# Attention and an ELU feed-forward layer on one core: weights loaded and decoded in pairs, and the first 64 queries of a pair turned by DMA

## The chip, the cores and the metric

The kernel runs on one core of one Trainium2 chip. The metric is the device time of one execution in microseconds; times of the kernel before are the median of three runs. Beside them there is one profiled execution, recorded by the hardware profiler, from which all durations below come.

## The reference

```python
def _attn_ref(q, k, v, s):                       # q, k, v: 8 batches, 8 heads, 576 positions, 64 wide
    scores = (1.0 / np.sqrt(D)) * np.matmul(q, k.transpose(0, 1, 3, 2))
    causal = np.triu(np.ones((S, S), dtype=bool), k=1)
    cum = np.cumsum(np.maximum(s, 0.0), axis=-1)
    bias = -(cum[:, :, :, None] - cum[:, :, None, :])
    scores = np.where(causal, -1000000000.0, scores + np.minimum(bias, 0.0))
    scores = scores - np.max(scores, axis=-1, keepdims=True)
    attn = np.exp(scores)
    attn = attn / (np.sum(attn, axis=-1, keepdims=True) + 1e-09)
    return np.matmul(attn, v)
...
x = attn_out.transpose(0, 2, 1, 3).reshape(8 * 576, 512)     # 4608 tokens
h = x @ w_in                                                 # 512 x 2048
g = np.where(h > 0.0, h, np.exp(np.minimum(h, 0.0)) - 1.0)
return g @ w_out                                             # 2048 x 512
```

All inputs are float32 and so is the output.

## The kernel before, in words

**The planner.** The program does not write its instructions in the order in which they run. It hands operations to a small planner (class `Plan`): each operation has a priority, its reads and writes, and one or more ways, that is an engine with an assumed cost. `issue` then takes, again and again, the operation that could start first by its own reckoning (ties by priority), chooses the way that ends first, and appends the instruction to that engine's program. So the order on every engine is fixed when the kernel is built, and each engine works it off in order. An operation's buffer is part of the reckoning: it cannot start before a slot of its pool is free. Until a planned time of 60 us (`FILL_T`) PE's gaps are filled by transpositions of the identity into a scratch bank (L1545, L1547).

**Three parts of the work.**

1. *Low units.* For batches 0 to 2, each of the four head pairs' first 320 positions are done in float32 products (`scoring_low` and `weighing_low`; tiles `sc`, `pl`, `trl`, `tl`, `avl`). Their x feeds the feed-forward layer's chunk 0.
2. *Later pairs.* The rest of the attention is done by `Unit`s with operands that are split into two float16 parts. A pair of heads has a unit for its first 64 queries ("None" in the names, both heads in one 128-row block; 20 of these in all) and one for each head's later queries. For a head's unit: scores (L1065), maximum and exponential (L1068 on DVE, L1073 on ACT), probabilities scaled and split in two parts (`halved`, L1119 to L1133), a DMA transposition T<-p (L409, issued on SP's queue), products with v (L1252: the two heads of a pair stand side by side, each 64 columns of the array), and an eviction with a scale (L1264 on ACT or L1266 on DVE) into x, which is stored to `x_dram`.
3. *The feed-forward layer*, 18 chunks of 256 tokens. Chunk 0 takes float32 products and the decoded weights `wa` (first layer L1423, second layer L1477); the other 17 take float16 parts, three products for each (first layer L1427, second L1484), from the split weights `wp`. A first-layer tile h covers two blocks of 128 hidden units; gg is its activation.

**The None units before the change.** The probabilities are normalised in float32 (`normalize`, L1086 to L1090: psh), transposed on PE (L1218: tr_None), split into two rounded parts (`split_pt`: copy L443 or L444, difference L1151), multiplied with the values' two rounded parts side by side (L1211, two products of 128 columns: av_None), and brought to x by four half evictions (`halves`: copies L443 or L444, additions L1280), two for each head.

**The weights.** They arrive as 64-bit words, a float32 in 8 bytes. `load_unit` takes one block of 128 hidden units of one matrix, 512 KB, in one of four slots of `raws` (32 loads, w_in and w_out in turn). Decoding is an ACT pass over the one half-word (L693), a mask on the other (L697 on DVE or L699 on ACT), and their union on DVE (L702: `wa`), then a maximum (L623 on DVE or L626 on ACT: `peaks`). After the last of them `weight_scales` makes the scales of both matrices, and `split_unit` makes the two parts of each block (the scaled high part L428 to L430; the low part L717 on DVE), at a priority of −500, ahead of nearly everything.

**Around it.** T has two buffers of its own, and two more where the last groups of `wa` lay once these are free. Score tiles may use the h banks while no more than the first nine h tiles have been opened. A later pair's operands are loaded, scaled, split, written to DRAM (`spread`) and read again (`set`). SP issues every one of these DMAs in one queue.

## Time and profile before

| | |
|---|---|
| median of the runs | 1038.81 us (1037.28 to 1039.48) |
| the profiled execution | 1034.6 us, of which its span 1032.8 us |
| PE busy | 1003.1 us, 97% of the span |
| DVE, ACT, POOL busy | 845.2 (82%), 669.0 (65%), 295.9 (29%) us |
| largest groups on PE | first layer 402.7 + 297.3 us, second layer 392.7 us (float16 parts; they overlap) |
| DMA moved | 179.83 MB, mean 174 GB/s |

Busy times are those of one profiled execution. A row of groups gives line, engine, operation and tiles, the count, then busy time and the mean of one in ns, and after the second bar the engine's idle time ahead of them and who ended it. PE's matmuls are pipelined, so a matmul's duration is longer than the distance to the next one; what one costs is read from the starts. "128*64" is the part of the array that is used. In the views PEld is the weight load, SPq a queue's issue.

### The profile page before, as it was taken

The numbers are of one execution on the slowest core, as the hardware profiler recorded it, in microseconds if no ns is written. First come the engines' busy times: TensorE is split into PE (matmuls) and PEld (weight loads), VectorE is DVE, ScalarE is ACT, GpSimd is POOL, SyncE is SP. The second block draws the span as 40 slices with busy tenths as digits, with TensorE's granted clock in tenths as the row PEclk, the third lists the DMA queues.
The fourth block names the chain that finished last, engine by engine and source line by source line (L and its number), as shares of the span: only waits on it lengthen the run. The fifth ranks groups of instructions, "written<-read, shape, count | busy, mean of one in ns | idle before, by whom it ended". The sixth has DMA issues, their size and how long they took to land. (4 is left out here: it accounts for less than half of the span.)

```text
span 1032.8 us, 21782 instructions
## 1 busy us (share of the span) xinstructions
PE 1003.1 (97%) x7305; PEld 688.7 (67%) x7305; DVE 845.2 (82%) x2346; ACT 669.0 (65%) x1559; POOL 295.9 (29%) x487
## 2 busy tenths in 40 slices
PE   8889999999999999999999999999999999999998
PEld 6667656676666666666666666676666676666665
DVE  7999998788988988898889999798988898863232
ACT  4898755666667766776776766666675765644343
POOL 6343452242323323241234242222232123100000
PEclk9999999999999999999999999999999999999999
DMA  7997524589979997999989987979998998841000
GB/s 197 276 289 236 150 72 95 124 190 213 222 166 212 207 192 165 198 202 208 196 174 201 232 179 174 229 181 192 215 198 196 227 202 187 182 94 47 1 21 21
DMA packets 296724, 179.83 MB, mean 174 GB/s; under 512 B 209908, under 2 KB 270564, under 8 KB 296612
## 3 DMA queue, kind: packets, MB, share of 16 engines
q1 hardware_dynamic: 296612, 178.45, 75.7%
q8 instruction: 57, 0.93, 0.4%
q14 instruction: 55, 0.45, 0.2%
HBM read 93.08 MB, written 36.81 MB: 126 GB/s over the span
## 5 line engine op out<-in xcount | busy, mean ns | idle before, releaser
L1427 PE MATMUL h<-xh,wp 128*128 128x256 f16 x2176 | 402.7, 273 | 0.7 <-DVE gg L1466 0.7
L1484 PE MATMUL o<-wp,gg 128*128 128x512 f16 x1632 | 392.7, 380 | 0.5 <-DVE gg L1466 0.5
L1427 PEld LDWEIGHTS <-wp 128*128 128x128 f16 x3264 | 317.4, 98 | 69.7 <-issue 2.1
L1427 PE MATMUL h<-xl,wp 128*128 128x256 f16 x1088 | 297.3, 273 | 1.1 <-DVE xl L1403 1.1
L1484 PEld LDWEIGHTS <-gg 128*128 128x128 f16 x1632 | 157.7, 98 | 144.5 <-DVE gg L1466 1.0
L1073 ACT ACTIVATE p<-p,mn 128x192 f32<-128x192 f32 (+1 forms) x232 | 143.7, 620 | 54.9 <-DVE mn L1068 52.9
L1133 DVE SCALAR_TENSOR_TENSOR p<-p,sm,p 128x512 f16<-128x512 f32 (+3 forms) x257 | 162.8, 662 | 4.9 <-POOL p L1125 2.4
L1459 DVE SCALAR_TENSOR_TENSOR h<-g,cs,h 128x512 f32<-128x512 f32 x136 | 102.0, 750 | 60.5 <-ACT g L1446 59.2
L1125 POOL TENSOR_SCALAR p<-p,sm 128x512 f16<-128x512 f32 (+3 forms) x94 | 65.1, 696 | 290.5 <-DVE sm L1079 117.1
L1439 ACT ACTIVATE g<-h,cs 128x512 f32<-128x512 f32 x136 | 92.8, 682 | 78.0 <-PE h L1427 77.2
L1463 ACT ACTIVATE gg<-h 128x512 f16<-128x512 f32 x132 | 78.3, 593 | 83.2 <-DVE h L1459 79.3
L1068 DVE CUSTOM_DVE_ANT_0 p<-sc,maskw 128x192 f32<-128x192 f32 (+1 forms) x232 | 109.5, 481 | 11.9 <-PE sc L1065 8.5
L1065 PE MATMUL sc<-set 128*128 128x288 f16 (+3 forms) x544 | 112.7, 299 | 4.5 <-DVE mn L1068 4.3
L1466 DVE SCALAR_TENSOR_TENSOR gg<-h,gg 128x512 f16<-128x512 f32 x136 | 93.3, 686 | 16.3 <-ACT gg L1463 15.7
L1129 ACT ACTIVATE p<-p,sm 128x512 f16<-128x512 f32 (+3 forms) x139 | 75.1, 557 | 19.0 <-DVE sm L1079 5.5
L1065 PEld LDWEIGHTS <-set 128*128 128x128 f16 x584 | 55.1, 98 | 41.6 <-issue 8.6
L1252 PE MATMUL av<-T,v 128*64 128x256 f16 (+5 forms) x960 | 62.4, 278 | 2.8 <-DMA T<-p 2.8
L1252 PEld LDWEIGHTS <-v 128*64 128x64 f16 x960 | 48.5, 110 | 23.3 <-issue 12.3
L1446 ACT ACTIVATE g<-g 128x512 f32<-128x512 f32 x81 | 50.9, 628 | 1.9
L428 POOL TENSOR_SCALAR v<-va,scales 128x320 f16<-128x320 f32 (+1 forms) x45 | 26.8, 599 | 64.9 <-PE av L1252 58.3
L1073 ACT ACTIVATION_READ_ACCUMULATOR p<-p,mn 128x1 f32 x232 | 43.7, 188 | 0.0
L1068 DVE CUSTOM_DVE_ANT_0 p<-sc,maskw,mn 128x288 f32<-128x288 f32 x64 | 32.9, 514 | 7.1 <-PE sc L1065 5.5
(200 smaller groups left out, 1261.0 us busy)
## 6 DMA issues: line engine op xcount, KB each, us to landing
set<-spread SPq DMA_DIRECT2D x32, 432.0 KB
spread<-parts_None SPq DMA_DIRECT2D x32, 288.0 KB
set<-spread SPq DMA_DIRECT2D x32, 288.0 KB
raws<-in_w_in_dram SPq DMA_DIRECT2D x16, 512.0 KB
raws<-in_w_out_dram SPq DMA_DIRECT2D x16, 512.0 KB
out_dram<-ost SPq DMA_DIRECT2D x32, 256.0 KB
va<-in_vb_dram SPq DMA_DIRECT2D x16, 352.0 KB
xc<-x_dram SPq DMA_DIRECT2D x22, 256.0 KB
```

Source lines behind the costliest of these rows:

```text
L1065: pe_.matmul(view(sc.v[:, :cw]), l, r, start=n == 0, stop=n == len(pairs) - 1)
L1068: op(prio, [("DVE", 84 + dve_p(cw), lambda i=i, sc=sc: dve.tensor_tensor_reduce(pt.v[:, i * cw : (i + 1) * cw], sc.v[:, :cw], mv(i * cw, c ...
L1073: op(prio, [("ACT", 480 + w / 1.2, lambda: act.activation(pt.v[:, :w], pt.v[:, :w], AF.Exp, bias=mn.v[:, n - 1 : n], scale=-1.0, accum_out ...
L1129: ("ACT", 295 + size / 1.2, lambda part=part: act.activation(part(0), own(part), AF.Copy, scale=sm.v[:, r])),
L1133: ("DVE-SB", dve_2(size), lambda part=part: dve.scalar_tensor_tensor(part(1), own(part), sm.v[:, r], part(0), ALU.mult, ALU.subtract)),
L1252: pe_.matmul(av.v[w.h * HB : (w.h + 1) * HB, dst], w.values.v[:, w.h, kb, v], part(w, kb, m), start=kb == 0 and m == 0 and v == 0, stop=kb ...
L1427: pe_.matmul(columns(k), weight_part(f, 0, part)[1]()[:, c * P : (c + 1) * P], xx.v[:, c], start=(c == 0 and m == 0), stop=(c == NCB - 1 a ...
L1439: op(side, [("ACT", act_c(W) + (0 if native else 90), lambda: act.activation(g.v, hp.v, AF.Exp, scale=1.0 if native else by(3)))], [hp] + ...
L1459: op(side, [("DVE", dve_p(W), lambda: dve.scalar_tensor_tensor(hp.v, g.v, by(2 if sign[0] else 1), hp.v, ALU.mult, ALU.max))], [g, cs], [hp])
L1463: ("ACT", act_c(W), lambda: act.activation(gg.v[:, 0], hp.v, AF.Copy, scale=2.0**-DOWN)),
L1466: op(side, [("DVE", dve_p(W), lambda: dve.scalar_tensor_tensor(gg.v[:, 1], hp.v, 2.0**-DOWN, gg.v[:, 0], ALU.mult, ALU.subtract))], [hp, ( ...
L1484: pe_.matmul(acc[i].v, gg.v[:, g, at], weight_part(f, 1, part)[1](), start=(f == 0 and m == 0), stop=(f == NF - 1 and m == 2),)
```

## The change

Two things are changed, with what goes along.

*Weights.* `load_pair` loads two blocks of one matrix at a time (1 MB, 16 loads) into one of four separate tiles, so up to 4 MB are under way; the decoding's passes, the maxima and the splits are 1024 wide instead of 512. The first loads no longer wait for a load of the second Low unit (`urgent` is gone). Each matrix has its own scale as soon as its own maxima are there, and a chunk's scales are made in two steps, for the first layer and for the output. The splits come at a priority of 130 and on instead of −500, that is behind the Low units. `wa` and `wp` are kept per matrix; T's two borrowed buffers are now the first two groups of w_out's `wa`. Score tiles may use the h banks until x's first split tile `xh` is opened. The key sums of all of batch 0's pairs come straight from `aux`.

*None units.* The probabilities are normalised and split into float16 parts (ph), transposed by a DMA (th, on SP's queue), and multiplied with float16 parts of the values by six products on half the array's width (`front_step`, three for each head). This is done where the same pair's later queries are weighed. For 16 of the 20 units the products go to a bank of their own (avh) with an eviction of 64 columns; for 4 into the av bank of the later queries, and x is evicted with these together.

The core of the diff:

```diff
+LAG, RATE, RAW = 1800.0, 225.0, 5
+W0, WD = 25, 6
+W_PAIRS = 3, 3, 2
-N_NATIVE, N_RAW = 1, 4
+N_NATIVE, PRIO_SPLIT = 1, 130
+W_GAP, S_GAP = 400.0, 0.0
...
+    def split_scaled(prio, n, dst, src, by, used, parts):
+        scaled(prio, n, lambda: dst(0), src, by, used, [(parts, 0)])
+        op(prio, [("DVE-SB", dve_2(n), lambda: dve.scalar_tensor_tensor(
+            dst(1), src(), by(), dst(0), ALU.mult, ALU.subtract))], [*used, (parts, 0)], [(parts, 1)])
...
-    raws = plan.buf(sb, [P, N_RAW, 512, 2], U32, "raws", tag=w_parts[0].key[1])
-    def load_unit(f, kind, src):
-        prio = W0 + WD * f
+    raws = [plan.buf(sb, [P, 2 * 512, 2], U32, f"raw_{g}", tag=w_parts[NG + g].key[1]) for g in range(NG)]
+    def load_pair(p, kind):
+        prio, n = W0 + WD * p, 2 * 512
...
-            load(prio, lambda: raws.v[:, slot].rearrange("p (a n) t -> p a (n t)", a=a),
-                 lambda: src.bitcast(U32), [], [(raws, (slot, 0)), (raws, (slot, 1))], P * 4096,
-                 urgent if f >= N_FREE else ())
+            load(prio, lambda: slot.v.rearrange("p (a n) t -> p a (n t)", a=a),
+                 lambda: src.bitcast(U32), [], [(slot, 0), (slot, 1)], P * n * RAW)
...
-    def split_unit(f, kind):
-        prio, col = -500 + f, slice(kind, kind + 1)
-        scaled(prio, 512, high_v, value, lambda: scales.v[:, col], [place, (scales, 0)], [high])
+    def split_pair(p, kind):
+        prio, col = PRIO_SPLIT + p, slice(kind, kind + 1)
+        scaled(prio, 2 * 512, high_v, value, lambda: scales.v[:, col], [place, (scales, kind)], [high])
...
-                        others=[("h", N_H, opening(1 + N_NATIVE * NFP)), ("o0", 1, opening(1)), ("o1", 1, opening(1))])
+                        others=[("h", N_H, lambda taken, key: not taken[xh.key]), ("o0", 1, opening(1)), ("o1", 1, opening(1))])
...
-                normalize(prio, psh, P, sm, 0)
+                split_scaled(prio, P, lambda m: p16.v[:, m], lambda: psh.v, lambda: sm.v[:, :1],
+                             [sm, (psh, "data")], p16)
+                turned_load(prio, 2, lambda: u.pt.v, lambda: p16.v.rearrange("p m q -> p (m q)"),
+                            [(p16, 0), (p16, 1)], [u.pt])
...
-                op(prio, [("PE", 111.0, lambda: pe_.transpose(tr.v[:, :P], u.pp.v, ident))],
-                   [(u.pp, "data")], [tr])
-                pieces = split_pt(prio, u.tag, tr, P)
-                products(pe(P), [
-                    ([pc, u.vs], lambda pc=pc, m=m: (
-                        u.vs.v.rearrange("p n a d -> p n (a d)")[:, 0], pc[0].v[:, m]))
-                    for m, pc in enumerate(pieces)], slice(P), True, True)
-                for h in range(2):
-                    halves(prio, h, HB, u.x_part((h, 0)), 0, av, h * HB)
...
+            if front is not None:
+                fav = av if c0 else any_bank(f"avh_{u.tag}")
+                def front_step():
+                    for m, v in ((0, 0), (1, 0), (0, 1)):
+                        for h in range(2):
+                            pe_.matmul(
+                                fav.v[h * HB : (h + 1) * HB, :HB], front.vs.v[:, v], front.pt.v[:, m, h * HB : (h + 1) * HB],
+                                start=m == 0 and v == 0, stop=v == 1,
+                            )
+                op(prio, [("PE", 120.0, front_step)], [front.pt, *[(w.pt, i) for w in pair for i in u.blocks],
+                                                       (front.vs, 0), (front.vs, 1)], [fav])
+                if not c0:
+                    evicted(HB, lambda: x.v[:, :HB], lambda: fav.v[:, :HB], [fav], [(x, "first")])
...
+        op(side, [("DVE-SB", 480.0, steps)],
+           [(scales, 0)] + [(scales, c) for c in cols if c > 3], [(cs, "in")])
+        op(side, [("DVE-SB", 120.0, lambda: dve.tensor_scalar(
+            cs.v[:, 4:5], cs.v[:, 3:4], scales.v[:, 3:4], 2.0**DOWN, ALU.mult, ALU.mult))],
+           [(scales, 3), (cs, "in")], [(cs, "out")])
```

How the planner's order moves is seen at three places. First PE at the end of the Low units, before: avl_3 are the last Low unit's products, h and o chunk 0's float32 products.

```order
L873 MATMUL avl_3_1570<-tl_3_1513,vs_128 64x64 x2
L1423 MATMUL h_4_1507<-x_0_1_891,wa_1001 128x256
L1477 MATMUL o_0_1272<-wa_672,gg_3_1468 128x512 x2
L1477 MATMUL o_1_1329<-wa_672,gg_3_1468 128x512 x2
...
L1477 MATMUL o_0_1272<-wa_1343,gg_7_1799 128x512 x2
L1477 MATMUL o_1_1329<-wa_1343,gg_7_1799 128x512 x2
L1427 LDWEIGHTS wp_1618
L1427 MATMUL h_0_1824<-xh,wp_1618 128x256
...
L1218 MATMUL tr_0_None_1843<-ident,psh_0_None_1679 128x128
```

And with the change:

```order
L857 MATMUL avl_3_1425<-tl_3_1356,vs_128 64x64 x2
L1452 MATMUL o_1_1410<-wa_0_484,gg_0_1288 128x512
L1398 MATMUL h_2_1461<-x_0_0_668,wa_0_410 128x256 x2
L1398 MATMUL h_2_1461<-x_0_1_802,wa_0_410 128x256 x2
...
L1452 MATMUL o_0_1359<-wa_2_1719,gg_7_1800 128x512 x2
L1452 MATMUL o_1_1410<-wa_2_1719,gg_7_1800 128x512 x2
L1402 LDWEIGHTS wp_0_1777
L1402 MATMUL h_0_1829<-xh,wp_0_1777 128x256
```

More of chunk 0's float32 products stand behind the last Low unit: from the third h tile on instead of the fifth, from the first gg on instead of the fourth. The first 64-query unit's transposition no longer stands in the first float16 tile h_0.

Second, DVE just ahead of that float16 tile, before:

```order
L1403 SCALAR_TENSOR_TENSOR xl<-xc_1_900,cs_1624,xh 128x512
L1455 SCALAR_TENSOR_TENSOR gg_7_1799<-h_7_1760,g_7_1790 128x512
L717 SCALAR_TENSOR_TENSOR wp_1700<-wa_1001,scales,wp_1700 128x512 x4
L936 SCALAR_TENSOR_TENSOR v_0_0_0_1605<-va_147,scales,v_0_0_0_1605 128x3x64
...
L1078 TENSOR_SCALAR sm_0_None_1724<-sm_0_None_1724 128x1
L1079 RECIPROCAL sm_0_None_1724<-sm_0_None_1724 128x1
```

And with the change:

```order
L1378 SCALAR_TENSOR_TENSOR xl<-xc_1_809,cs_1771,xh 128x512
L1430 SCALAR_TENSOR_TENSOR gg_7_1800<-h_7_1750,g_7_1787 128x512
...
L711 SCALAR_TENSOR_TENSOR wp_0_1777<-wa_0_410,scales,wp_0_1777 128x1024
L428 COPY ost_0_1822<-o_0_1359 128x512
L711 SCALAR_TENSOR_TENSOR wp_0_1777<-wa_0_410,scales,wp_0_1777 128x1024
L711 SCALAR_TENSOR_TENSOR wp_1_1796<-wa_0_410,scales,wp_1_1796 128x1024
...
L1441 SCALAR_TENSOR_TENSOR gg_0_1911<-h_0_1829,gg_0_1911 128x512
```

The weights' low parts (wp) now follow the last float32 activation gg_7 instead of standing partly ahead of it, and the first None unit's reciprocal (sm_0_None), which stood behind eight such splits and value splits, has gone from this place to one much earlier.

Third, PE at a None unit's products, before:

```order
L1427 MATMUL h_0_1824<-xh,wp_1618 128x256
L1211 MATMUL av_0_None_1886<-pc_0_None_1855,vs_0_None_1334 128x128
L1427 LDWEIGHTS wp_1618
L1427 MATMUL h_0_1824<-xh,wp_1618 128x256
```

And with the change, a unit of the 16 with a bank of their own:

```order
L1402 MATMUL h_0_3126<-xh,wp_0_1777 128x256
L1223 LDWEIGHTS vs_0_None_2114
L1223 MATMUL avh_0_1_0_3135<-th_0_None_2761,vs_0_None_2114 64x64
...
L1402 LDWEIGHTS wp_0_1777
L1402 MATMUL h_0_3126<-xh,wp_0_1777 128x256
```

The six products, each with its weight load, stand together between two first-layer products.

More of the change, by code (lines that the diff above doesn't have):

```diff
@@ L93 @@
 class Op:
-    __slots__ = ("ways", "after", "before", "behind", "bufs", "new", "prio", "ready", "left", "filler")
+    __slots__ = ("ways", "after", "before", "behind", "bufs", "new", "prio", "ready", "left", "filler", "gap")
 class Plan:
@@ L235, in issue @@
                         for key, bufs, *rule in b.others:
-                            if rule and not rule[0](taken[key]):
+                            if rule and not rule[0](taken, key):
                                 continue
@@ L705, in load_unit @@
         else:
             load(prio, lambda: value().rearrange("p (a n) -> p a n", a=a), lambda: src,
-                 [], [place], P * 2048, urgent)
-        peak(prio, 512, value, [place], (A_IN, A_OUT)[kind] + f,
-             aside=(lambda: raw(0).bitcast(F32)) if wide else None, also=[(raws, (slot, 0))] if wide else [])
-    def split_unit(f, kind):
-        prio, col = -500 + f, slice(kind, kind + 1)
-        place, value = weight(f, kind)
-        (high, high_v), (low, low_v) = (weight_part(f, kind, m) for m in range(2))
-        scaled(prio, 512, high_v, value, lambda: scales.v[:, col], [place, (scales, 0)], [high])
-        op(prio, [("DVE-SB", dve_2(512), lambda: dve.scalar_tensor_tensor(
-            low_v(), value(), scales.v[:, col], high_v(), ALU.mult, ALU.subtract))],
-           [place, (scales, 0), high], [low])
@@ L721, in load_weights @@
-    def load_weights(f0, f1):
-        wi = w_in.rearrange("(c p) f -> p c f", p=P)
-        wo = w_out.rearrange("(f p) (a m) -> f p a m", p=P, a=1)
-        for f in range(f0, f1):
-            fs = slice(f * P, (f + 1) * P)
-            load_unit(f, 0, wi[:, :, fs])
-            load_unit(f, 1, wo[f])
+                 [], [place], P * n * 4)
+        peak(prio, n, value, [place], (A_IN, A_OUT)[kind] + p,
+             aside=(lambda: raw(0).bitcast(F32)) if wide else None, also=[(slot, 0)] if wide else [])
@@ new lines, in split_pair @@
+    def split_pair(p, kind):
+        prio, col = PRIO_SPLIT + p, slice(kind, kind + 1)
+        place, value = weight_pair(p, kind)
+        (high, high_v), (low, low_v) = (weight_part(2 * p, kind, m) for m in range(2))
+        scaled(prio, 2 * 512, high_v, value, lambda: scales.v[:, col], [place, (scales, kind)], [high])
+        op(prio, [("DVE-SB", dve_2(2 * 512), lambda: dve.scalar_tensor_tensor(
+            low_v(), value(), scales.v[:, col], high_v(), ALU.mult, ALU.subtract))],
+           [place, (scales, kind), high], [low])
@@ L1246, in heads, with evicted @@
         def heads():
+            x, label = u.x_part(("rows", first))
+            back = slice(u.back, u.back + 1)
+            def evicted(n, dst, src, reads, writes):
+                op(prio, [
+                    ("ACT", act_c(n) + 90, lambda: act.activation(dst(), src(), AF.Copy, scale=scales.v[:, back])),
+                    ("DVE", dve_p(n), lambda: dve.tensor_scalar(dst(), src(), scales.v[:, back], None, ALU.mult)),
+                ], [*reads, (scales, u.back)], writes)
+            if front is not None:
[11 more added lines that the diff above has]
+                    evicted(HB, lambda: x.v[:, :HB], lambda: fav.v[:, :HB], [fav], [(x, "first")])
             def step():
                 for kb in range(last + 1):
-                    dst = slice(wq - columns(kb), wq)
+                    dst = slice(c0 + wq - columns(kb), c0 + wq)
                     for m, v in ((0, 0), (1, 0), (0, 1)) if kb < last else ((0, 0), (0, 1)):
@@ L1260, in heads @@
                [av])
[L1261 to L1268 removed]
+            cols = slice(HB + P * first - c0, HB + P * first + wq)
+            evicted(c0 + wq, lambda: x.v[:, cols], lambda: av.v[:, : c0 + wq], [av], [(x, label)])
             load(prio, lambda: x_dram.v[u.b, u.j][:, u.cols], lambda: x.v[:, u.cols], [x],
@@ L1517, in output @@
             ]
-            op(side, [w for w in ways if only is None or w[0] in only], reads + [cs], writes)
+            op(side, [w for w in ways if only is None or w[0] in only], reads + [(cs, "out")], writes)
         for i in range(NTB):
```

201 lines of the change are left out of this document (83 added, 118 removed).

## The prediction

> **What bounds the kernel now.** First the page's busy times, then the same by stage (windows; columns: length, then PE, PEld, DVE, ACT, POOL busy with counts, PE clock, DMA share, GB/s).
>
> ```profile
> span 1032.8 us, 21782 instructions
> PE 1003.1 (97%) x7305; PEld 688.7 (67%) x7305; DVE 845.2 (82%) x2346; ACT 669.0 (65%) x1559; POOL 295.9 (29%) x487
> ```
> ```profile
> 0.00:60.00 60.00, 51.56 (x342) 39.69 (x343) 50.29 (x150) 41.81 (x125) 30.43 (x72) 0.97 0.86 245
> 60.00:123.00 63.00, 60.25 (x344) 43.34 (x343) 57.20 (x192) 50.69 (x151) 18.73 (x49) 1.00 0.80 235
> 123.00:152.00 29.00, 28.60 (x97) 17.23 (x97) 28.48 (x64) 18.81 (x38) 18.30 (x19) 1.00 0.18 60
> 152.00:160.00 8.00, 5.87 (x39) 4.43 (x37) 6.94 (x24) 4.13 (x8) 5.06 (x7) 0.79 0.48 143
> 172.00:930.00 758.00, 745.93 (x5719) 509.61 (x5718) 658.92 (x1846) 506.06 (x1156) 220.96 (x338) 1.00 0.88 191
> 26.00:52.00 26.00, 23.03 (x158) 16.62 (x156) 23.73 (x82) 21.84 (x65) 8.52 (x23) 1.00 0.93 278
> ```
>
> PE is the bound: idle for 1032.8 − 1003.1 = 29.7 us. Of these 8.4 lie in the first 60 us, 2.8 and 0.4 in the next two rows, 2.1 in 152 to 160, 12.1 in 172 to 930; the rest in short stretches and the tail. DVE is nearly full from 60 to 152 (57.2 of 63, 28.5 of 29), and yet PE hardly waits there, for the native products of the first layers stand between. So the large DVE saving of this change can be paid out only in PE's idle time or in PE work that goes; both are small. Where PE waits after 60 us (waits: total, times, longest), and the first DVE-bound stall on PE's, DVE's and ACT's timelines:
>
> ```profile
> PE sc L1065 <- DVE mn L1068: 5.5, 11, 1.0
> PE av L1252 <- DMA T<-p: 2.8, 3, 1.8
> ```
> ```profile
> 152.64 0.27 PE L1427 MATMUL h<-xh,wp 128*128 128x256 f16 x1
> 155.04 0.43 PE L1218 MATMUL tr_None<-ident,psh_None 128*128 128x128 f32 x1 [2.13 <-ACT psh_None L1090]
> 156.23 0.42 PE L1427 MATMUL h<-xh,wp 128*128 128x256 f16 x1
> 156.44 0.42 PE L1427 MATMUL h<-xl,wp 128*128 128x256 f16 x1
> ```
> ```profile
> 148.09 4.80 DVE L717 SCALAR_TENSOR_TENSOR wp<-wa,scales,wp 128x512 f16<-128x512 f32 x4
> 152.81 1.48 DVE L936 SCALAR_TENSOR_TENSOR v<-va,scales,v 128x192 f16<-128x192 f32 x4
> 154.39 0.16 DVE L1079 RECIPROCAL sm_None<-sm_None 128x1 f32<-128x1 f32 x1
> ```
> ```profile
> 154.58 0.40 ACT L1090 ACTIVATE psh_None<-psh_None,sm_None 128x128 f32<-128x128 f32 x1 [3.06 <-DVE sm_None L1079]
> ```
>
> This is one chain: four weight splits and four value splits on DVE, then the reciprocal of the first 64-query unit, its normalising on ACT, its transposition on PE. PE stands for 2.1 us, and then runs at half speed (0.21 us from one product to the next at 156.23; 0.11 in the rows at 181.09 below): the clock in that window is 0.79, so (1 − 0.79) × 8 = 1.7 us more. The stall costs 3.8 us.
>
> **The change part by part.**
>
> *Weights in pairs, DVE's share.* The groups (busy, mean ns | idle before), and the eviction row that stands in two widths:
>
> ```profile
> L717 DVE SCALAR_TENSOR_TENSOR wp<-wa,scales,wp 128x512 f16<-128x512 f32 x32 | 25.0, 832 | 0.0
> L702 DVE SCALAR_TENSOR_TENSOR wa<-raws 128x512 uint32<-128x512 uint32 x32 | 22.4, 703 | 1.0 <-ACT raws L693 0.3 <-DVE raws L697 0.2
> L697 DVE TENSOR_SCALAR raws<-raws 128x512 uint32<-128x512 uint32 x29 | 13.0, 451 | 0.8 <-DMA raws<-in_w_in_dram 0.8
> L623 DVE TENSOR_REDUCE peaks<-wa 128x1 f32<-128x512 f32 x18 | 12.2, 679 | 0.1
> L1266 DVE TENSOR_SCALAR x<-av,scales 128x256 f32<-128x256 f32 x8 | 3.9, 481 | 1.5 <-PE av L1252 1.5
> L1266 DVE TENSOR_SCALAR x_None<-av,scales 128x512 f32<-128x512 f32 (+1 forms) x7 | 4.7, 672 | 2.6 <-PE av L1252 2.6
> ```
>
> 256 columns more cost 0.672 − 0.481 = 0.19 us, so 512 more cost 0.38 (estimate from the last two rows): a 1024-wide split 1.21, a decode 1.08, a mask 0.83, a peak 1.06. Splits go from 25.0 to 16 × 1.21 = 19.4, decodes from 22.4 to 17.3, masks from 13.0 to 9 × 0.83 = 7.5, peaks from 12.2 to 4 × 1.06 = 4.2: DVE −24 us, all before the f16 products or just at their start (a part of it goes to ACT, which the first rows show at 0.65 to 0.8 of its time). What that gives PE: at most the idle time of those stages.
>
> *The splits' place.* They no longer come before everything as soon as the scale is known. In the new order the first 64-query unit's reciprocal stands some 70 DVE instructions ahead of the first product in f16, and PE no longer turns its probabilities at all. So the chain at 152 goes: −3.8. What is late next: the first f16 products want the splits of the first w_in pairs, and DVE's new order has them just behind the last native activation, one after the other with the output evictions between. Cover is PE's native work left behind the last Low product, which the order raises to six first-layer and seven second-layer pairs (before: about four, and five). If that covers the splits, 0 comes back; if the first f16 product waits for two splits and the eviction between, 1.21 + 0.7 + 1.21 = 3.1 comes back (half speed behind it not counted). I take 1.3, the lower half, since the row 123:152 shows DVE keeping up with PE while it still did 4.8 us of splits in a block. **Term: −2.5 (−3.8 to +1).**
>
> *Native work moved behind the Low units.* It is the same work; idle in 60 to 152 is 3.2 in all, so the gain is 3.2 at most. The loss: with less native work between, the Low chain (score, maximum, exponential, transposition) stands barer. DVE's and ACT's sums ahead of the last Low score fall by about a fifth, PE's sum there too. **Term: 0 (−3 to +3).**
>
> *Loads of 1 MB, four at once.*
>
> ```profile
> 17.55 0.59 SPq L404 DMA_DIRECT2D raws<-in_w_in_dram  x1
> 20.30 0.51 SPq L404 DMA_DIRECT2D raws<-in_w_out_dram  x1
> ACT L626 <- DMA vs<-in_vb_dram: 8.2, 1, 8.2
> ```
>
> Four loads of 0.5 MB leave SP from 17.55 to 20.30, 2.1 MB, which take 7.5 us at the 278 GB/s of 26 to 52; four of 1 MB take 15.1. Behind them stand the key sums of batch 0's last pair, the queries and the values of batch 1. They can come up to 7.5 us later; ACT already once waits 8.2 us for values. Against that, four Low units of batch 0 are loaded ahead of the burst, and the order fills PE with as many transpositions of the identity as before, plus four (4 × 0.11 = +0.4). 16 issues fewer on SP (−8 us of a queue with room). **Term: +0.4 (−4, half of the idle time, to +7.5).**
>
> *The first 64 queries of a pair.* Old PE work:
>
> ```profile
> L1218 PE MATMUL tr_None<-ident,psh_None 128*128 128x128 f32 x20 | 5.8, 292 | 3.6 <-ACT psh_None L1090 2.1 <-POOL psh_None L1086 1.5
> L1211 PE MATMUL av_None<-pc_None,vs_None 128*128 128x128 f32 x40 | 9.6, 312 | 0.9 <-ACT x_None L1264 0.6 <-DVE x_None L1266 0.3
> 207.82 0.27 PE L1427 MATMUL h<-xh,wp 128*128 128x256 f16 x1
> 207.85 0.42 PE L1211 MATMUL av_None<-pc_None,vs_None 128*128 128x128 f32 x2
> 208.11 0.28 PE L1427 MATMUL h<-xh,wp 128*128 128x256 f16 x1
> 181.09 0.27 PE L1427 MATMUL h<-xl,wp 128*128 128x256 f16 x1
> 181.20 0.27 PE L1427 MATMUL h<-xh,wp 128*128 128x256 f16 x1
> 181.40 0.83 PE L1252 MATMUL av<-T,v 128*64 128x256 f16 x16
> 182.16 0.28 PE L1427 MATMUL h<-xh,wp 128*128 128x256 f16 x1
> ```
>
> By starts, two av_None products put 208.11 − 207.82 = 0.29 between products that otherwise stand 0.11 apart: 0.18. The transposition, one instruction of that form, I set at half, 0.09: 20 × 0.27 = 5.4 us goes. New are six half-width products for each unit, two heads side by side. The nearest row is the av group: from 181.20 to its start is 0.20 instead of 0.11, an entry of 0.09, and 16 products (8 pairs, mostly 256 columns wide) last 0.76, 0.095 a pair. Three pairs of 64 columns cost between 3 × 0.095/4 = 0.07 and 3 × 0.095 = 0.29; with the entry 0.16 to 0.38. I take 0.28, near the middle. In 16 of the 20 the order puts the group alone between first- or second-layer products, in 4 next to the pair's own av group, where there is no entry (0.1): 16 × 0.28 + 4 × 0.1 = 4.9. **Term: −0.5 (−2.6 to +1.1).**
>
> The Trainium skill, "TensorEngine Tiling (Array Packing)", section "Key Properties", says that changing the tiling mode drains TensorE; the entry of 0.20 instead of 0.11 agrees. By the rule each isolated group pays on both sides; were the exit another 0.09, the low end of 0.16 would be 0.25, and the term −0.9 instead of −2.6 at best: a rule that speaks against the 16 isolated groups.
>
> Waits of that path: the groups' 3.6 + 0.9 us, of which 2.1 are the stall above, so 2.4 remain. The new products come an exponential, a split and a DMA after the score, but late in the order: their units' rows stand well ahead. **Term: −2 (−2.4 to +1.5).** DVE: the half evictions, the subtractions and the copies behind PE's transposition go, two short splits and some 64-column evictions come; about −6 us net over the kernel (8.8 + 5.6 + 3.8 = 18.2 against 20 × (0.28 + 0.22) + 8 × 0.22 = 11.8), from these rows:
>
> ```profile
> L1280 DVE TENSOR_TENSOR x_None<-av_None,x_None 64x64 f32<-64x64 f32 x40 | 8.8, 219 | 1.2 <-ACT x_None L443 0.5
> L1151 DVE TENSOR_TENSOR pc_None<-tr_None,pc_None 128x128 fp32r<-128x128 f32 x20 | 5.6, 282 | 0.5 <-ACT pc_None L443 0.5
> L444 DVE COPY x_None<-av_None 64x64 f32<-64x64 f32 x17 | 3.8, 221 | 3.3 <-DMA x_dram<-x_None 2.1 <-ACT x_None L443 0.8
> ```
>
> DVE was 0.87 full from 172 to 930, and PE's 5.5 us for the maxima show it late eleven times; 6 of 659 us is 1%. **Term: −1.5 (−4 to 0).**
>
> *Twenty more DMA transpositions.*
>
> ```profile
> L409 SPq DMA_TRANSPOSE T<-p x168: 1206/1309/4601, 172.6 to 922.4; - x168
> ```
>
> 20 × 1.3 = 26 us more of SP's queue, and of the blocks that the order has turned, 1480 become 1520 (+2.7%) in a stage whose DMA share is 0.88. Everything that SP issues later stands behind them. PE's 2.8 us for T can grow. **Term: +0.5 (0 to +5).**
>
> *Sum:* −2.5 + 0 + 0.4 − 0.5 − 2 − 1.5 + 0.5 = −5.6. The profiled execution took 1034.6, so 1029.0; the median of the runs is 1038.8, 4.2 above it, so **1033.2 us** for a median.
>
> **The rivals.** *A, DVE really is the bound of the early stages.* For: DVE at 57.2 of 63 and 28.5 of 29. Against: PE is as full, and the count of filling transpositions does not fall. Then the stall goes whole (−3.8), half of the first 60 us' idle (−4), the 3.2 of 60 to 152, the 64-query waits (−2.4) and half of the maxima (−2.7): −16, so 1023. *B, PE is the bound and its waits only change names.* For: of 29.7 us idle only two kinds of wait beside the stall are over 2 us; each engine's order is fixed by a planner, not by what comes first. Then the sum keeps the stall's −2.5, loses the −2 and −1.5, pays +1 at the switch and +1 for the groups: −1, so 1038. *C, the burst:* the Low loads come 7.5 us late, and ACT and DVE, whose orders are fixed, stand before a raw block with Low work behind it. PE's idle in the first 60 us rises from 8.4 to 15.9: +7.5 − 2.5 − 0.5 − 1.5 = +3, so 1042. It decides once that idle passes 8.4 + 4.5, what the other terms bring. *D, transpositions through SP:* +5 in 172 to 930 and the units' waits kept, +1: 1040.
>
> **How the numbers follow.** Chances: forecast 0.45, A 0.13, B 0.17, C 0.17, D 0.08. The range holds A's end and C's: 1022 to 1043; the forecast's own is 1029 to 1037. A measurement of this kernel can tell about 0.2% from no change, 2.1 us, so faster is below 1036.7. Faster: 0.40 of the forecast, A, 0.07 of B: 0.60. Slower: C's 0.14, 0.05 of D, 0.03 of B: 0.22. The same: 0.18.
>
> **What would show it.** Right: no wait over 1 us at the first f16 product, and the clock at 1.00 there; PE's idle before that point at 12 to 16 us; h-to-h distance around an isolated group near 0.39 us; transpositions still 1.3 us; DVE's busy time near 815. Wrong: PE waiting in the first 60 us for kl, queries or values (C); waits for th or T above 5 us (D); more than 2 us before the first f16 product for wp, which would put the stall back under another name.

## The result, and the profile after

The changed kernel takes 1045.2 us (median of nine runs) against 1037.3 of the kernel before on the same chip. One of the nine runs took 5902.75 us; without it the median is 1043.9 us and the ratio 1.0065, with a 95% interval of 1.0046 to 1.0083. It is slower by 0.65%, some 7 us; the forecast was 1033 in a range that ended at 1043. The profiled execution agrees: its span is 1039.8 us, 7.0 more.

Busy times on the page of the changed kernel, and its windows as they were shown of before:

```profile
span 1039.8 us, 21744 instructions
PE 1005.3 (97%) x7374; PEld 685.1 (66%) x7374; DVE 833.5 (80%) x2270; ACT 664.7 (64%) x1493; POOL 252.0 (24%) x431
```
```profile
0.00:60.00 60.00, 48.11 (x319) 37.00 (x320) 43.58 (x121) 38.95 (x106) 27.77 (x69) 0.97 0.81 254
123.00:152.00 29.00, 28.11 (x115) 17.95 (x113) 19.93 (x36) 17.89 (x30) 1.75 (x4) 1.00 0.84 236
150.00:167.00 17.00, 13.21 (x42) 6.99 (x41) 15.24 (x40) 11.17 (x15) 3.82 (x3) 0.90 0.10 30
172.00:930.00 758.00, 746.96 (x5779) 508.42 (x5778) 666.04 (x1825) 503.00 (x1131) 197.94 (x298) 1.00 0.87 189
```

DVE did become less busy, by 11.7 us (forecast 30), and PE is idle for longer, 34.5 us instead of 29.7. From 172 to 930 nothing is lost: 11.0 us idle instead of 12.1. The loss lies before that. The first float16 product, from which on the two kernels do the same work, starts at 166.4 us instead of 151.8. Only 1.5 us of these 14.7 is work that has been moved ahead of it.

PE's idle time in the first 60 us went from 8.4 to 11.9. What ended it is told by two rows on PE's timeline of the changed kernel:

```profile
26.45 0.81 PE L1050 MATMUL sc<-kl,low_queries 128*128 128x320 f32 x2 [1.81 <-DVE mn L1053]
32.76 0.79 PE L1050 MATMUL sc<-kl,low_queries 128*128 128x128 f32 x4 [1.96 <-DMA low_queries<-in_qT_dram]
```

Behind the first stand ACT and DVE, whose programs have a decoding pass ahead of Low work:

```profile
23.49 1.19 ACT L687 ACTIVATE raw<-raw 128x1024 f32<-128x1024 f32 x1 [1.61 <-DMA raw<-in_w_in_dram]
25.02 0.56 ACT L1058 ACTIVATE pl_both<-pl_both,mn 128x320 f32<-128x320 f32 x1
25.70 0.17 DVE L1063 TENSOR_SCALAR sml<-sml 128x5 f32<-128x5 f32 x1 [1.51 <-ACT pl_both L1058]
```

ACT stands 1.6 us before the first megabyte, decodes for 1.2, and only then does the exponential that DVE's row sum and PE's next scores wait for. The second row is a Low load that lands late: its queries left SP at 28.80 and PE could use them at 32.76.

The other place is the switch from float32 to float16 products. PE's rows there (idle and releaser in brackets), and SP, ACT, DVE and POOL ahead of them; the row alone at the end is the last weight load of the kernel before:

```profile
153.03 0.49 PE L650 MATMUL flat<-ident,tops 128*128 128x128 f32 x2 [1.92 <-DVE tops L639]
161.20 5.40 PE L1452 MATMUL o<-wa,gg 128*128 128x512 f32 x8 [1.87 <-DVE gg L1430]
```
```profile
137.71 0.59 SPq L402 DMA_DIRECT2D raw<-in_w_out_dram  x1
143.40 1.18 ACT L687 ACTIVATE raw<-raw 128x1024 f32<-128x1024 f32 x1 [2.23 <-DMA raw<-in_w_out_dram]
150.10 0.69 DVE L691 TENSOR_SCALAR raw<-raw 128x1024 uint32<-128x1024 uint32 x1 [0.68 <-DMA raw<-in_w_out_dram]
150.91 0.68 ACT L618 ACTIVATE junk<-stq_None 128x576 bf16<-128x576 f32 x1 [1.62 <-DMA stq_None<-in_qT_dram]
154.38 1.21 DVE L696 SCALAR_TENSOR_TENSOR wa<-raw 128x1024 uint32<-128x1024 uint32 x1
156.85 3.16 POOL L414 TENSOR_SCALAR wp<-wa,scales 128x1024 f16<-128x1024 f32 x2
157.24 5.29 ACT L415 ACTIVATE wp<-wa,scales 128x1024 f16<-128x1024 f32 x5
157.77 1.26 DVE L1425 TENSOR_SCALAR g<-g 128x512 f32<-128x512 f32 x1
158.95 1.59 DVE L1378 SCALAR_TENSOR_TENSOR xl<-xc,cs,xh 128x512 f16<-128x512 f32 x1
160.47 0.68 DVE L1430 SCALAR_TENSOR_TENSOR gg<-h,g 128x512 f32<-128x512 f32 x1
```
```profile
107.01 0.33 SPq L404 DMA_DIRECT2D raws<-in_w_out_dram  x1
```

The last weight load leaves SP at 137.7 us; before, the last one left at 107.0. So decoding, scale, splits and the last float32 activations come together in 20 us, on engines that work in a fixed order. PE waits 1.9 us for a scale and 1.9 for the last activation. Ahead of the scale, ACT also stood 1.6 us before a later pair's queries (`stq_None`), with the last maximum that the scale needs behind them. After the second wait the array runs at half speed again: three second-layer products start 0.42 us too late each, the ones beside them by less, and a granted clock of 0.90 in 150 to 167 makes (1 − 0.90) × 17 = 1.7 us. After the first wait, which was as long, the granted clock stayed at 1.00 (153 to 161). The stall that was to go has come back under another name, and larger: 5.5 us instead of 3.8.

**POOL beside DVE.** Two of the DVE rows above, L1425 and L1378, stand just ahead of the last activation and are long, and POOL splits weights beside them. In this trace 49 rows of L1425 have no POOL instruction beside them and take 0.41 to 0.43 us; 15 such rows of L1378 take 0.74 to 0.75. So the two took 1.7 us longer than that, nearly all of the wait of 1.9. The old stall shows the same. POOL was at work there from 144.08 on:

```profile
144.08 7.60 POOL L539 TENSOR_SCALAR_AFFINE_SELECT set<-set 64x1152 f16<-64x1152 f16 x3
```

Of the four splits in 4.80 us that the prediction shows, three took 1.03 to 1.63 us, against 0.73 to 0.75 for the 19 splits without POOL beside them: 2.1 us more, for a wait of 2.13. In both traces the DVE instructions that take over 1.2 times the undisturbed median of their kind all but 0.1 us have POOL beside them; what they take more is 33 us over the whole kernel, before and after alike. The planner does keep the two engines' work apart (`PORT_LEAD`), but in its own reckoned time. This is read from the rows; no run here takes POOL's work away. As the sum is the same in both kernels, it explains the two stalls and not the slower total.

**An account by starts.** To compare kernels with different orders, I take for every product on PE the median distance from its start to the next one's, by its kind and shape, over all kernels here. The sum of these is the work; what a stretch takes beyond its work and its filling transpositions is lost. A 64-query unit is set at its measured 0.29 us (old) or, alone between other products, 0.31 (new). Up to the first float16 product the kernel before loses 21.7 us and fills 15.4, together 37.1; the changed one loses 34.4 and fills 15.9, together 50.3. After it they lose 26.5 and 20.3. So: +13.2 before the switch, −6.2 behind it, −0.4 in the new groups, together +6.6 of the 7.0. Of the 12.7 us more that are lost before the switch, 8.7 are behind float32 first- and second-layer products, 3.9 behind filling transpositions; the Low units' own rows give none.

### The profile page after: what moved, and what is told of

It reads as the page before. It is cut to its first block, busy times and chain, and to the rows that moved or that the text cites. A ratio compares the mean times of both kernels' runs of the same rounds, so it can differ in the third digit from the quotient of the medians.

```text
span 1039.8 us, 21744 instructions
## 1 busy us (share of the span) xinstructions
PE 1005.3 (97%) x7374; PEld 685.1 (66%) x7374; DVE 833.5 (80%) x2270; ACT 664.7 (64%) x1493; POOL 252.0 (24%) x431
## 5 line engine op out<-in xcount | busy, mean ns | idle before, releaser
L1118 DVE SCALAR_TENSOR_TENSOR p<-p,sm,p 128x512 f16<-128x512 f32 (+3 forms) x253 | 156.1, 644 | 7.5 <-ACT p L1114 5.4
L1434 DVE SCALAR_TENSOR_TENSOR h<-g,cs,h 128x512 f32<-128x512 f32 x136 | 101.9, 750 | 58.7 <-ACT g L1421 57.3
L1110 POOL TENSOR_SCALAR p<-p,sm 128x64 f16<-128x64 f32 (+3 forms) x104 | 71.7, 695 | 282.0 <-DVE sm L1064 119.0
L1053 DVE CUSTOM_DVE_ANT_0 p<-sc,maskw 128x192 f32<-128x192 f32 (+1 forms) x232 | 108.9, 480 | 11.2 <-PE sc L1050 7.6
L1421 ACT ACTIVATE g<-g 128x512 f32<-128x512 f32 x73 | 45.8, 627 | 1.8
L1425 DVE TENSOR_SCALAR g<-g 128x512 f32<-128x512 f32 x71 | 34.7, 488 | 11.4 <-ACT g L1414 10.9
L1050 PE MATMUL sc<-kl,low_queries 128*128 128x192 f32 (+2 forms) x110 | 30.8, 384 | 8.5 <-DVE mn L1053 3.2
```

Of the source, the lines that this page charges most:

```text
L1050: pe_.matmul(view(sc.v[:, :cw]), l, r, start=n == 0, stop=n == len(pairs) - 1)
L1053: op(prio, [("DVE", 84 + dve_p(cw), lambda i=i, sc=sc: dve.tensor_tensor_reduce(pt.v[:, i * cw : (i + 1) * cw], sc.v[:, :cw], mv(i * cw, c ...
L1118: ("DVE-SB", dve_2(size), lambda part=part: dve.scalar_tensor_tensor(part(1), own(part), sm.v[:, r], part(0), ALU.mult, ALU.subtract)),
L1434: op(side, [("DVE", dve_p(W), lambda: dve.scalar_tensor_tensor(hp.v, g.v, by(2 if sign[0] else 1), hp.v, ALU.mult, ALU.max))], [g, (cs, "i ...
```

## The experiments

Three theories were set against each other. **Theory 1**: the weights half loses the time before the first float16 product. **Theory 2**: the 64-query half loses it, by its DMA transpositions and isolated groups. **Theory 3**: neither, but the planner's order, which any edit draws anew. In all runs the kernel before stood beside, at 1036.9 to 1038.1 us; ratios are to it. "Early" is the sum of lost and filling time on PE before the first float16 product, "late" what is lost after it, by the account above (before: 37.1 and 26.5). Both come from one profiled execution of each kernel, while the runs of one kernel spread by up to 12 us (gap100: 1040.6 to 1052.5).

**One half each.** w_only has the changed weights and the old 64-query units; none_only the reverse.

```diff
 w_only, against the changed kernel
-                split_scaled(prio, P, lambda m: p16.v[:, m], lambda: psh.v, lambda: sm.v[:, :1], ...
-                turned_load(prio, 2, ...
+                normalize(prio, psh, P, sm, 0)
...
-                def front_step():
+            def pair():
+                op(prio, [("PE", 111.0, lambda: pe_.transpose(tr.v[:, :P], u.pp.v, ident))], ...
```

> The weights half of the change alone; the 64-query units as in the kernel before. Theory 1 (the loss lies in the first 170 us: decode and native products run late): the first float16 product starts at 165 to 168 us as in the whole change, and the kernel is slower than the whole change by what the new 64-query units saved, some 4 us: 1047 to 1050, against 1037 before. Theory 2 (the 64-query units' DMA transpositions and isolated products cost the time): 1033 to 1036.

Measured: 1043.0 us, ratio 1.0053 (1.0028 to 1.0078); first float16 product at 161.5; early 48.6, late 23.1. The early loss is there as theory 1 says; the first product comes earlier and the total is below what it expected.

> The 64-query half alone, on the kernel before; weights as before. Theory 1: first float16 product at 150 to 156 us, the stall of 2.1 us behind it gone, 1031 to 1035 against 1037 before. Theory 2: 1041 to 1046.

Measured: 1044.7, ratio 1.0073 (1.0048 to 1.0099). Theory 2's number. But it is not early (40.1): late 31.3, in single waits, as the views of PE's waits from 170 to 930 us show (total, times, longest):

```profile
PE av L1258 <- DMA T<-p: 5.9, 5, 2.7
PE sc L1070 <- DVE mn L1073: 4.3, 8, 1.1
PE h L1421 <- ACT xh L429: 2.9, 1, 2.9
```

Each half alone is as slow as both together, so the halves do not add up; that speaks for theory 3 as well, and the next runs go to it.

**Another draw of the order.** The same instructions, with one assumption of the planner changed by half a per cent:

```diff
-LAG, RATE = 1800.0, 225.0
+LAG, RATE = 1790.0, 225.0
```

> The kernel before with one of the planner's assumptions changed by half a per cent (a DMA's assumed latency 1790 instead of 1800 ns): the same instructions, another order. It measures what the planner's order alone is worth. Theory 3 (scatter): it differs from 1037 by 3 us or more. Theories 1 and 2 (a mechanism in one half of the change): within 2 us of 1037.

> As the run with 1790, with 1810 ns. Scatter: 3 us or more from 1037, on either side. A mechanism: within 2 us.

> The 64-query half alone with the assumed latency at 1790 ns. If the 64-query path itself costs 7 us: 1042 to 1047 again, with waits for T above 4 us. If its 1044.7 was a bad draw of the order: 1033 to 1040, the single stalls of 3 us at 362 and 840 gone.

> The whole change with the assumed latency at 1790 ns. Late weights are in this order too (the first 64 weight-independent rows are the same), so theory 1 expects the first float16 product at 165 to 168 us again and 1042 to 1048; scatter alone would allow 1037 to 1050.

> The whole change with a DMA's assumed latency at 1810 instead of 1800 ns, a third draw of its order. From two draws (1045, 1062) and three of the kernel before (1037, 1044, 1051): 1042 to 1062. Before the first float16 product PE should again lose 49 us or more to waits and fillings, as in the two draws known, against 38 to 46 before.

| | ratio (95%) | us | first f16 product | early | late |
|---|---|---|---|---|---|
| before, 1800 | 1 | 1037.3 | 151.8 | 37.1 | 26.5 |
| before, 1790 | 1.0062 (1.0038 to 1.0087) | 1043.7 | 152.4 | 37.7 | 32.7 |
| before, 1810 | 1.0138 (1.0102 to 1.0174) | 1051.0 | 160.3 | 44.8 | 32.9 |
| none_only, 1800 | 1.0073 (1.0048 to 1.0099) | 1044.7 | 155.5 | 40.1 | 31.3 |
| none_only, 1790 | 1.0070 (1.0044 to 1.0097) | 1043.9 | 156.5 | 41.1 | 31.3 |
| w_only, 1800 | 1.0053 (1.0028 to 1.0078) | 1043.0 | 161.5 | 48.6 | 23.1 |
| changed, 1800 | 1.0065 (1.0046 to 1.0083) | 1043.9 | 166.4 | 50.3 | 20.3 |
| changed, 1790 | 1.0238 (1.0195 to 1.0282) | 1061.6 | 164.1 | 51.4 | 42.6 |
| changed, 1810 | 1.0145 (1.0119 to 1.0172) | 1052.4 | 166.4 | 53.7 | 31.3 |

Both draws of the kernel before are what theory 3 expected. The changed kernel's draw at 1790 is not what either theory expected (164.1 and 1061.6); its draw at 1810 is. Two things follow. The planner's order alone is worth 6 to 14 us to the kernel before and 8 to 18 to the changed one: both at 1800 are the best of their three draws. The 7 us between them are no more than that, so the total of this pair alone says little about the mechanism (theory 3). But the early column does not mix: 37 to 45 us in the five orders with the old weights, 49 to 54 in the four with the new ones. The weights half costs about 11 us there (means 40.2 and 51.0), in every draw (theory 1). Where the line is drawn does not make this difference: 20 us of work later, behind the old stall, the sums are 41 to 45 us with the old weights and 53 to 57 with the new ones. The late column scatters from 20 to 43 with the new weights and from 27 to 33 with the old; in the worst draw PE waits 13.4 us for the maxima behind DVE:

```profile
PE sc L1050 <- DVE mn L1053: 13.4, 10, 4.2
PE av L1238 <- DMA T<-p: 5.0, 3, 2.0
```

Theory 2 is not borne out as a mechanism, though both draws of the 64-query half give its total, with waits for T of 5.9 and 4.3 us, which at 1790 is just what the first expectation asked for: their late loss (31.3, 31.3) is what the kernel before loses in its own other draws (32.7, 32.9), with waits for T of 3.9 and 4.3 and without the new path. That the other draw would be back at 1033 to 1040 was a miss; two draws do not exclude a cost of a few us.

**What in the weights half.** First the burst, the prediction's slower rival: two raw tiles in turn instead of four.

```diff
-            slot = raws[(2 * p + kind) % NG]
+            slot = raws[(2 * p + kind) % 2]
```

> The whole change, but only two raw tiles of 1 MB in turn, so 2 MB under way at first as in the kernel before. If the burst of 4 MB delays the Low units' loads (the rival of the prediction): PE's idle in the first 60 us falls from 11.9 to about 8.5 and the time to 1041 or 1042. If late weights are the cost: loads come later still, first float16 product after 170 us, 1047 to 1055.

Measured: 1055.9, ratio 1.0175 (1.0155 to 1.0194). PE's idle in the first 60 us falls from 11.9 to 9.8, so about 2 us there may be the burst's, no more; but the loads come later still (the last leaves at 165 us, first float16 product at 182.0), and PE waits 13.4 us for decoded weights and 8.8 for activations:

```profile
PE o L1452 <- DVE wa L696: 13.4, 2, 7.2
PE o L1452 <- DVE gg L1430: 8.8, 5, 3.4
```

Then the holding back: in the change the planner ranks a weight operation as if it began 400 ns later. 100 ns, none, none on the decoding (gap_load), none on the loads (gap_dec):

```diff
-W_GAP, S_GAP = 400.0, 0.0
+W_GAP, S_GAP = 100.0, 0.0
```

> The whole change, but the planner holds a weight operation back by 100 ns instead of 400 when others could start; 24 instead of 16 native first-layer steps then stand before the last Low product. Theory 1, that the holding back starves the native work: the last decode some 15 us earlier, 1036 to 1041. If the place of the decode does not matter (the 1 MB pieces themselves cost it): within 2 us of the whole change, 1043 to 1047.

> The whole change without any holding back of weight operations (0 instead of 400 ns). The first four loads then stand ahead of the Low units' in SP's queue, and 201 filling transpositions instead of 146 are in PE's program. If late weights are what the first stage loses: first float16 product at 150 to 158 us. If the 4 MB burst in front of the Low units' operands costs: PE's idle plus filling before the first float16 product above 51 us, first float16 product after 166.

> The whole change, holding back only the loads, not the decoding. If held-back decoding is the cost, PE's unused and filling time before the first float16 product falls from 51 to 40 to 46 us. If it is the loads, it stays at 50 or more.

> The whole change, holding back only the decoding, not the loads; 208 filling transpositions. If held-back decoding is the cost: 50 us or more of unused and filling time before the first float16 product. If the loads: 40 to 46.

| | ratio (95%) | us | first f16 product | early | late |
|---|---|---|---|---|---|
| gap100 | 1.0086 (1.0059 to 1.0113) | 1046.1 | 162.9 | 44.9 | 24.6 |
| gap0 | 1.0156 (1.0123 to 1.0190) | 1053.0 | 176.6 | 58.6 | 22.6 |
| gap_load | 1.0142 (1.0107 to 1.0177) | 1051.5 | 176.8 | 58.8 | 22.7 |
| gap_dec | 1.0153 (1.0120 to 1.0190) | 1052.7 | 174.3 | 57.3 | 24.6 |

Of the last three there are two runs each, and of half_load and frame_old_g100 below. Held-back weights are not the whole cause: without holding back, or with only one of the two held back, the early loss is larger still, so these runs single out neither the loads nor the decoding. With 100 ns it is 5.4 us smaller, and the last load leaves at 113.5 us instead of 137.7, though the whole kernel is no faster: 1046.1 is what was expected if the decode's place does not matter. gap_load shows why early decoding does not help. Its first load leaves at 17.45 us, as in the change, and on ACT, DVE and PE stands:

```profile
24.02 1.17 ACT L689 ACTIVATE raw<-raw 128x1024 f32<-128x1024 f32 x1 [2.46 <-DMA raw<-in_w_in_dram]
24.02 0.69 DVE L693 TENSOR_SCALAR raw<-raw 128x1024 uint32<-128x1024 uint32 x1 [3.15 <-DMA raw<-in_w_in_dram]
25.63 1.01 PE L1052 MATMUL sc<-kl,low_queries 128*128 128x192 f32 x2 [3.78 <-DVE mn L1055]
```

A megabyte lands 6.6 us after its issue; two engines stand before it, and PE's next scores behind both. In the first 170 us ACT and DVE wait 1.4 us for raw blocks in the kernel before, 9.4 in the changed one, 11.2 in gap_load. gap0 and gap_dec instead put the first four loads ahead of the Low units' operands in SP's queue.

Is it the size of a load, or the width of a decoding pass? half_load loads each megabyte in two halves; half_dec does the three decoding passes in halves.

```diff
+            for m in range(2):
+                load(prio, lambda half=half: half(slot.v.rearrange("p (a n) t -> p a (n t)", a=a)),
+                     lambda half=half: half(src.bitcast(U32)), [], [(slot, (0, m)), (slot, (1, m))], P * n * RAW / 2)
```

> The whole change, each 1 MB loaded in two pieces of 0.5 MB, decoded 1024 wide as in the change. If the size of a load costs the first stage: PE's unused and filling time before the first float16 product falls from 51 us to 40 to 46. If not: 48 to 55.

> The whole change with 1 MB loads, the three decoding passes done in halves of 512 columns (maxima and splits stay 1024 wide). If the wide passes cost by standing in front of the Low units' exponentials and maxima on ACT and DVE: 40 to 46 us unused and filling before the first float16 product. If not: 48 to 55.

Measured: 1046.6 (1.0098, 1.0060 to 1.0136) with early 52.8, and 1046.3 (1.0086, 1.0058 to 1.0114) with early 50.3. Neither alone is it. Both together were not tried.

The bunch at the switch: holding back for the first four of eight pairs only.

```diff
-            plan.gap = W_GAP
+            plan.gap = W_GAP if p < 4 else 0.0
```

> The whole change, with weight operations held back by 400 ns only for the first four pairs and not for the last four. If the last loads' late start (137 us) and the bunch of decoding, scale, splits and activations behind them make the waits at 150 and 159 us: the last load leaves before 115 us, the first float16 product starts at 148 to 158, both waits are gone, and the kernel takes 1034 to 1042. If early weights only move the loss into the Low units, as in the runs with no holding back: first float16 product after 166.

Measured: 1050.6, ratio 1.0132 (1.0093 to 1.0171); early 50.8, first float16 product at 167.5. The waits at 150 and 159 us are gone, but the last load still leaves at 133 us and not before 115, and the same time is lost between the Low units, as the second expectation had it.

**The surroundings.** frame_old puts the kernel before's rules around the 1 MB pieces: no weight load before the key sums of the second Low unit, sums over DRAM, decay parts after the second unit, h banks until the ninth tile. frame_new puts the change's rules, except that for the h banks, around the old pieces, on none_only.

```diff
 frame_old, against the changed kernel
+            load(prio, ..., [(slot, 0), (slot, 1)], P * n * RAW, urgent)
-            if u is todo[NP - 1][0]:
+            if u is todo[1][0]:
-                        others=[("h", N_H, lambda taken, key: not taken[xh.key]), ...
+                        others=[("h", N_H, opening(1 + N_NATIVE * NFP)), ...
```

> The whole change, with what stands around the weights as in the kernel before: the first weight load waits for the key sums of the second Low unit, key sums of the later ones over DRAM, decay parts after the second unit, score tiles in h banks until the ninth h tile. Pieces of 1 MB, four slots, holding back by 400 ns stay. If the pieces themselves (1 MB, 1024 wide, in fixed order with the Low units) cost: 48 to 55 us of unused and filling time before the first float16 product, as in the whole change (51). If the surroundings cost: 38 to 46.

> The 64-query half alone, weights in pieces of 0.5 MB as before, but with the change's surroundings: no load waits for the second Low unit (the first four then stand ahead of the Low units' operands in SP's queue), key sums of batch 0 directly, decay parts after the fourth unit. If the place of the first loads is what costs: 48 us or more unused and filling before the first float16 product (41 without these surroundings). If not: 40 to 44.

> As the first of these three, holding back by 100 ns instead of 400; the later weight loads move forward by some ten places in SP's queue. If a mean holding back with the old surroundings is what the 1 MB pieces need: 38 to 46 us unused and filling, 1035 to 1042. If not: 46 to 55.

| | ratio (95%) | us | first f16 product | early | late |
|---|---|---|---|---|---|
| frame_old | 0.9975 (0.9952 to 0.9999) | 1036.4 | 166.2 | 49.6 | 16.1 |
| frame_new | 1.0106 (1.0086 to 1.0126) | 1048.3 | 160.4 | 48.4 | 25.2 |
| frame_old_g100 | 1.0122 (1.0073 to 1.0172) | 1050.5 | 157.0 | 43.9 | 33.7 |

frame_old loses as much early as the change: held back by 400 ns, the pieces cost there whatever stands around them. frame_new loses 8.3 us more than none_only: the surroundings cost as well when the old pieces get them, with the first four loads ahead of the Low units' operands (the first leaves at 6.8 us; in the change it left at 17.4). Less holding back again takes 5.7 us off the early loss, as it took 5.4 before, and again the total does not follow, against what was expected (1035 to 1042): frame_old_g100 loses 33.7 late, frame_old 16.1. The total of frame_old, 0.25% below the kernel before with an interval that ends at 0.01%, is owed to the smallest late loss of all; with the scatter above, I take it as a good draw and not as a proof that its rules are better. It is the only one of these that does not lose to the kernel before.

## Why the prediction was wrong

**What bounds it, and where a gain can be had: right.** PE was and is the bound, DVE's saved time could be paid out only in PE's idle time. It was not seen that idle time can also grow.

**The chain at 152 us: the term −2.5 (−3.8 to +1) was wrong.** The chain itself went, as forecast: no wait for a 64-query unit's normalising is left. What "comes back" was taken as 1.3 and bounded by two splits and an eviction, 3.1. It was 1.9 + 1.9 + 1.7 us (half speed) before the first float16 product, and 1.2 us more in waits of second-layer products for wp and gg from 181 to 186. The step that failed is the cover: PE's native work left behind the last Low product was counted as hiding the splits, but this work itself needs DVE and ACT for its activations, and the scale's product stands in the midst of it. Both wait in DVE's and ACT's programs behind the decoding of weights that landed last and behind x's splits. More work behind the Low units was no cover; it was part of the bunch. The prediction also read the old stall as a matter of order alone; its rows show four splits that took 2.1 us longer beside POOL than undisturbed ones.

**Native work moved: 0 (−3 to +3).** By starts, 8.7 us more are lost behind float32 products, 5.5 of them the three items at the switch above. The other 3.2 are at the bound. The reasoning bounded the gain by idle time and the loss by nothing better than symmetry; the loads' later place in SP's queue, which they left until 137.7 us instead of 107.0, could have been read from the order and was not.

**Loads of 1 MB: +0.4 (−4 to +7.5).** Measured: the first native product starts 4.4 us later, of which 3.5 us is PE's idle in the first 60 us. That is rival C's mechanism, a decoding pass standing before a raw block with Low work behind it, inside the bound but ten times the value taken. raws2 leaves some 2 us for the burst itself.

**The 64-query units on PE: −0.5, right.** From start to start a group alone between first-layer products takes 0.42 instead of 0.11, 0.31 more (forecast 0.28), which is 5.0 for the 16; the old units cost 0.29 (forecast 0.27). By its own sizes, though, the term's low end is −2.4 and not −2.6, and with an exit −1.0 and not −0.9. The rows of a group:

```profile
259.64 0.27 PE L1402 MATMUL h<-xh,wp 128*128 128x256 f16 x1
259.85 0.28 PE L1223 MATMUL avh<-th_None,vs_None 128*64 128x64 f16 x6
260.06 0.28 PE L1402 MATMUL h<-xh,wp 128*128 128x256 f16 x1
```

The six products themselves start within 0.09 us of one another; what is paid is entry (0.20) and exit (0.13). The Trainium skill, "TensorEngine Tiling (Array Packing)", section "Key Properties", says that changing the tiling mode drains TensorE; entry and exit agree with it. By these rows 16 groups pay (0.20 + 0.13 − 0.11) × 16 = 3.5 us for the two.

**Behind the switch: −2 − 1.5 + 0.5 and the stall of 3.8, together −6.8; measured −6.2.** Right in this pair. The draws show how much of that was luck: in the changed kernel's other two orders the same terms came out at +16 and +5 us (late 42.6 and 31.3 against 26.5).

**The measured sum.** −3.8 + 5.5 at the switch, +3.2 for the native work, +4.4 for the loads, −0.4 for the groups and −6.2 + 3.8 = −2.4 for the rest behind the switch: +6.5 of the 7.0 us.

**The sizes on DVE were off.** A split takes 1.43 us (estimate 1.21), a decoding pass 1.23 (1.08), a maximum 1.21 (1.06), a mask 0.75 (0.83). The four groups went from 72.6 to 53.6 us, −19 instead of −24.

```profile
L711 DVE SCALAR_TENSOR_TENSOR wp<-wa,scales,wp 128x1024 f16<-128x1024 f32 x16 | 22.7, 1432 | 0.0
L696 DVE SCALAR_TENSOR_TENSOR wa<-raw 128x1024 uint32<-128x1024 uint32 x16 | 19.4, 1228 | 1.9 <-ACT raw L687 1.9
L691 DVE TENSOR_SCALAR raw<-raw 128x1024 uint32<-128x1024 uint32 x9 | 6.7, 749 | 4.5 <-DMA raw<-in_w_out_dram 3.8 <-DMA raw<-in_w_in_dram 0.7
L615 DVE TENSOR_REDUCE peaks<-wa 128x1 f32<-128x1024 f32 x4 | 4.8, 1212 | 0.0
```

The slope was misread. The row of 672 ns mixes two widths ("+1 forms"): five evictions of 512 columns and two of 256. Kept apart, the wide ones of the kernel before are

```profile
L1266 DVE TENSOR_SCALAR x_None<-av,scales 128x512 f32<-128x512 f32 x5 | 3.7, 747 | 1.7 <-PE av L1252 1.7
```

so 256 columns more cost 0.747 − 0.481 = 0.27 us and 512 more 0.53. With that the estimates are 1.23 for a decoding pass and 1.21 for a maximum, as measured; for a mask 0.98, too much. A split without POOL beside it went from 0.74 to 1.28, also 0.54 more; the mean of 1.43 holds three splits of 2.0 to 2.2 us beside POOL.

The rest of the forecast of 30 us was filled again, since the new order gives DVE work that other engines did (POOL is 43.9 us less busy): 71 instead of 63 activation passes, 34.7 instead of 28.8 us, and value splits of 42.9 instead of 30.1.

**The rivals.** C (1042, 0.17) was nearest, and its mechanism is in the trace; but it came with a second place, the switch, that no case had. B's items, added to the forecast's sum, give −0.1 and not −1. D did not happen: PE's waits for T fell from 2.8 to 0.5 us. What none of the cases held is that a new order alone moves this kernel by 6 to 18 us. With that, the range of 1022 to 1043 was too narrow on the slow side.

**Open.** The weights half, held back by 400 ns, costs some 11 us before the first float16 product in every draw. Shown is where (waits for raw blocks ahead of Low work, and the bunch at the switch) and that neither the burst, a load's size, a pass's width nor the surroundings alone is it; holding back by 100 ns takes about half of it away, in both surroundings, and no holding back at all adds to it. Why stays open. So does why the total does not follow the early loss. One candidate was not tried alone: the change lets the planner count 5 instead of 8 bytes for each value of a raw load, so that it may put decoding ahead of the data's landing.

## What to carry to other kernels

Where a planner fixes every engine's order, an edit is two changes: what the instructions cost, and a new draw of the order. Measure the second first, by moving an assumption that means nothing by half a per cent; here that was worth 0.6 to 1.7%, as much as the change or more. A slope wants rows of one shape each; the mean of a mixed group misled here. Read from the new order when each load leaves and what stands behind its first consumer, not only how much work is saved: an engine that works in order turns a late or larger load into a wait for everything behind it.

## What had not been expected of the hardware

A group of six half-width products alone between full-width ones costs 0.31 us, of which 0.22 is entry and exit: the switch is dearer than the work. A pass of 1024 columns on DVE saves little over two of 512: without POOL beside them two splits of 512 columns take 2 × 0.74 = 1.48 us, one of 1024 takes 1.28. Beside POOL the same splits took up to 1.63 and 2.16 us, which is more than the wider pass saves.
